# Hash attention and token/channel mixer on one core: where the second group of hash products of the first pair stands

## The chip, the cores and the metric

The kernel runs on one core of a Trainium2 chip. The metric is the device time of one execution in microseconds (us); the time before is the median of three runs, and the profile comes from one further execution. The engines are named as in the profile: PE is TensorE (PEld its weight loads), DVE is VectorE, ACT is ScalarE, POOL is GpSimd, SP is SyncE, which here only issues transfers.

## The reference

Attention with a hash mask over 4 batches, 8 heads, 768 positions and 64 channels per head, then a mixer over tokens and channels. A query sees a key only if all six signs of their projections agree:

```python
q_bits = (np.einsum('bhsd,dk->bhsk', q, proj) > 0).astype(np.int64)
k_bits = (np.einsum('bhsd,dk->bhsk', k, proj) > 0).astype(np.int64)
...
mask = q_bucket[:, :, :, None] == k_bucket[:, :, None, :]
scores = scale * np.matmul(q, k.transpose(0, 1, 3, 2))
scores = np.where(mask, scores, -1000000000.0)
scores = scores - np.max(scores, axis=-1, keepdims=True)
attn = np.exp(scores)
attn = attn / (np.sum(attn, axis=-1, keepdims=True) + 1e-09)
return np.matmul(attn, v).astype(np.float32)
...
h = np.maximum(xt @ w_tok1, 0.0) @ w_tok2
u = x + h.transpose(0, 2, 1)
h2 = np.maximum(u @ w_ch1, 0.0) @ w_ch2
return (u + h2).astype(np.float32)
```

## The kernel before

The program has three stages, one after the other: attention (to about 310 us in the profile), the token mixer, and the channel mixer, which takes more than half of the time. Each stage is written out by hand in the order in which its instructions are to stand in the engines' queues; no scheduler moves them. The change touches only the beginning of the attention.

Attention goes over 16 pairs: a pair is two heads of one batch, whose 64 channels each fill the 128 rows of the array, head i in rows 64i to 64i + 63. Queries are taken in two halves of 384 (class `Half`), keys in six blocks c of 128. For a half and a block, `product` (L350) makes the scores of both heads in one PSUM tile `sc`, of which there are three: the plain products of q and k in float32, and the bits products, which add a large negative number wherever the hashes of query and key differ. `exponential` (L358) then takes the exponential on ACT. The loop at L367 keeps its order by hand: within a half the plain products of a block come first and its bits products after. In the very first half (`first` is true) the plain products of blocks 0 and 1 are both issued before the bits products of block 0: block 0 is put on the list `waiting` and the loop goes on.

The bits come from hash products. From pair 1 on, `hashes(n)` (L292) makes them a pair ahead and moves them into place by DMA. For pair 0 there is no pair ahead, so `first_hashes(half)` (L318) makes them in place: four products of 32 columns (eight passes on TensorE, since float32 goes in two), then on DVE one comparison (L330), one scaling of the key bits (L331) and two comparisons that put the query bits in the rows of their heads (L334). `first_hashes(0)` reads positions 0 to 383 of q and k, which hold key blocks 0 to 2 and the queries of the first half. `first_hashes(1)` reads positions 384 to 767, which hold key blocks 3 to 5 and the queries of the second half. Both were issued at L365, ahead of all score products. They write to two different PSUM tiles (`acc` for the first, `sm` for the second).

The loads of pair 0 are three transfers on SP's queue (L271, twice, for the first half of k and of q; L272 for the second half of both), then follow the load of pair 1 (L268), the values of pair 0 (L280, L282) and a first piece of a weight (L169). Before any product on data stand twelve small products on constants (L469), whose result isn't used. An engine takes its instructions in order: one that waits for a load holds up those behind it.

Of the kernel before, what the change touches and what calls it, by code (L numbers as in the profile page):

```python
# [48 lines left out]
def kernel(  # L49
# [208 lines left out]
    def attention(pool, psum, W1, W2, x0):  # L258
# [59 lines left out]
        def first_hashes(half):  # L318

            sl = slice(HALF * half, HALF * half + HALF)  # L320
            ps = psum.tile([P, 512], F32, name="hw", tag="sm" if half else "acc", bufs=1)[:, :HALF]
            for i in range(2):
                for which in (1, 0):
                    at = D * i + 32 * (1 - which)
                    nc.tensor.matmul(  # L325
                        ps[at : at + 32], projwide[:, D * i : D * i + 32], loaded[0][0][:, which, sl],
                        start=True, stop=True,
                    )
            q, k = (bitrows[0][:, which, sl] for which in range(2))
            nc.vector.tensor_scalar(k, ps, 0.0, 0.5, op0=ALU.is_gt, op1=ALU.subtract)  # L330
            nc.vector.tensor_scalar(k, k, widescale, None, op0=ALU.mult)  # L331
            for i in range(2):
                at = D * i
                nc.vector.tensor_scalar(  # L334
                    q[at : at + 32], ps[at + 32 : at + 64], 0.0, 0.5, op0=ALU.is_gt, op1=ALU.subtract,
                )

        class Half:
# [5 lines left out]
            def scores(self):  # L344

                qkt, bits = loaded[self.n][0], bitrows[self.n % 2]
                qs = slice(HALF * self.half, HALF * self.half + HALF)
                first = self.n == self.half == 0

                def product(sc, t, c, start):  # L350
                    for i in range(2):
                        rows = slice(D * i, D * i + D)
                        nc.tensor.matmul(  # L353
                            sc[:, i, :HALF], t[rows, 1, P * c : P * c + P], t[rows, 0, qs],
                            start=start, stop=not start,
                        )

                def exponential(sc):  # L358
                    e = pool.tile([P, 2, HALF], F32, name="e", tag="e", bufs=12)
                    nc.scalar.activation(e, sc[:, :, :HALF], ACT.Exp, scale=SCALE)  # L360
                    self.es.append(e)

                waiting = []
                if first:
                    for half in range(2):  # L365
                        first_hashes(half)
                for c in range(NR):  # L367
                    sc = psum.tile([P, 2, 512], F32, name="sc", tag="sc", bufs=3)
                    if c == self.half == 0 and not first:
                        product(sc, bits, c, True)  # L370
                        product(sc, qkt, c, False)
                        exponential(sc)
                        continue
                    product(sc, qkt, c, True)
                    waiting.append((c, sc))
                    if first and c == 0:
                        continue
                    for c, sc in waiting:
                        product(sc, bits, c, False)
                        exponential(sc)  # L380
                    waiting = []
# [1092 lines left out]
```

## Time and profile before

| | us |
|---|---|
| median of three runs | 797.34 |
| the three runs | 796.74 to 799.93 |
| the profiled execution, its own time | 795.77 |
| its span, first to last instruction | 794.0 |
| scores of one half, both heads, on TensorE (six blocks) | 4.9 |
| one pair in the attention, pitch of the chain | 18.97 |
| exponential of one block, on ACT (L360) | 0.811 |

The span is shorter than the execution's own time by the 1.8 us that lie around the first and last instruction. The half's 4.9 us are half of the 9.80 us that the chain gives to 12 blocks of one pair, and the pitch is the distance of two such pieces (44.92 less 25.96, in us from the start of the span). Times in the profile are counted from the span's start. A row of the timeline stands for a run of like instructions, with its start, its length, its engine and line, and in brackets the idle time of the engine before it with what ended it. Matmuls overlap, so one row may begin before the row ahead of it has ended.

### The profile page before, as it was taken

Reading aid. Unit: us, or ns where it says so; the run is one execution under the profiler, and the core shown is the slowest. Engines: PE = TensorE matmul, PEld = TensorE weight load, DVE = VectorE, ACT = ScalarE, POOL = GpSimd, SP = SyncE. Lnnn points to the kernel's source line nnn. Section 1 sums busy time; section 2 is a strip of 40 time slices with the busy share of each in tenths; the row PEclk is TensorE's granted clock in tenths of the full one; section 3 lists DMA queues with packets and bytes.
Section 4 is the critical chain, followed back from the end, with each engine's and each line's share of the span. In section 5 each row is a group of like instructions: output and inputs, shape, how many; then the busy total and the mean of one; then the engine's idle time right before and its main releaser. Section 6 shows DMA issues by size and latency. Waiting matters only on the chain.

```text
span 794.0 us, 12166 instructions
## 1 busy us (share of the span) xinstructions
PE 786.4 (99%) x4661; PEld 464.9 (59%) x4661; DVE 659.7 (83%) x885; ACT 441.4 (56%) x706; POOL 53.5 (7%) x77
## 2 busy tenths in 40 slices
PE   8999999999999999999999999999999999999997
PEld 4444444444444444455544458876667886666886
DVE  5989898988987677999688788988769897778986
ACT  6688888888888886333323221327773335775111
POOL 1000000000000000011121010111110012000001
PEclk9999999999999999999999999999999999999999
DMA  4435353538352425796726994699754578730456
GB/s 163 163 123 163 123 163 123 163 122 246 143 178 87 154 47 166 215 281 173 175 60 228 334 356 145 185 294 283 218 148 139 217 204 195 218 109 1 148 176 159
DMA packets 90974, 138.67 MB, mean 175 GB/s; under 512 B 29656, under 2 KB 63392, under 8 KB 88608
## 3 DMA queue, kind: packets, MB, share of 16 engines
q1 hardware_dynamic: 82752, 112.86, 42.9%
q0 software_dynamic: 7728, 24.64, 14.0%
q8 instruction: 38, 0.62, 0.3%
q10 hardware_dynamic: 432, 0.34, 0.2%
q14 instruction: 24, 0.20, 0.1%
HBM read 97.21 MB, written 33.16 MB: 164 GB/s over the span
## 4 chain that ended last, share of the span: by engine, by line
PE 99%; DMA 1%; SPq 0%; DVE 0%; issue 0%
PE b L779 50%; PE sc L353 20%; PE acc L406 16%; PE t L652 5%; PE t L692 5%; PE sums L430 2%; PE hp L301 1%; DMA qk<-in_qk 1%; PE hw L325 0%; SPq L271 0%; DVE second L1202 0%; PE b L1319 0%; SPq L1469 0%
## 5 line engine op out<-in xcount | busy, mean ns | idle before, releaser
L360 ACT ACTIVATE e<-sc 128x768 f32<-128x768 f32 x192 | 154.1, 811 | 11.6 <-PE sc L353 11.2
L353 PE MATMUL sc<-qk 64*128 64x384 f32 x768 | 152.6, 483 | 0.0
L779 PE MATMUL b<-R,second 128*128 128x256 f32 (+1 forms) x612 | 150.9, 404 | 0.0
L779 PEld LDWEIGHTS b<-R,second 128*128 128x128 f32 x612 | 116.3, 190 | 31.6 <-issue 17.2
L785 ACT COPY c<-b 128x512 f32<-128x512 f32 (+1 forms) x78 | 37.4, 488 | 169.2 <-PE b L779 159.6
L406 PE MATMUL acc<-e,vn 128*32 128x384 f32 x1536 | 127.0, 486 | 0.0
L391 DVE TENSOR_TENSOR esd<-esd,e 128x768 f32<-128x768 f32 x96 | 92.0, 958 | 10.4 <-ACT e L360 0.5
L406 PEld LDWEIGHTS acc<-e,vn 128*32 128x32 f32 x1536 | 49.9, 110 | 73.9 <-issue 73.3
L353 PEld LDWEIGHTS sc<-qk 64*128 64x128 f32 x768 | 68.2, 187 | 40.8 <-issue 35.6
L779 PE MATMUL b<-XT,WC 128*128 128x256 f32 (+1 forms) x264 | 82.5, 456 | 0.0
L779 PEld LDWEIGHTS b<-XT,WC 128*128 128x128 f32 x264 | 50.2, 190 | 29.6 <-issue 25.1
L353 PE MATMUL sc<-bits 64*128 64x384 bf16 x384 | 62.5, 323 | 0.0
L387 DVE SCALAR_TENSOR_TENSOR esd<-e 128x768 f32<-128x768 f32 x32 | 30.6, 955 | 24.5 <-ACT e L360 24.5
L652 PE MATMUL t<-x,W 128*128 128x512 f32 x96 | 41.8, 593 | 0.0
L353 PEld LDWEIGHTS <-bits 64*128 64x128 bf16 x384 | 18.7, 94 | 33.0 <-issue 9.0
L712 POOL DMA_DIRECT2D XT<-second x8 | 9.9, 1232 | 386.0 <-DVE second L711 361.6
L451 ACT COPY rec<-rec 32x384 f32<-32x384 f32 x64 | 32.6, 510 | 5.0 <-DVE rec L445 4.2
L412 ACT ACTIVATE num<-acc,vsum 128x384 f32<-128x384 f32 x32 | 18.6, 581 | 29.8 <-PE acc L406 29.4
L779 PE MATMUL b<-XT,SW 128*128 128x256 f32 (+1 forms) x120 | 34.6, 422 | 0.0
L779 PE MATMUL b<-TA,WC 128*128 128x512 f32 x72 | 33.8, 592 | 0.0
L779 PE MATMUL b<-TA,SW 128*128 128x512 f32 x72 | 32.9, 592 | 0.0
L394 DVE TENSOR_TENSOR esd<-esd,e 128x768 f32<-128x768 f32 x32 | 30.5, 954 | 1.9
(217 smaller groups left out, 1129.3 us busy)
## 6 DMA issues: line engine op xcount, KB each, us to landing
second<-left SPq DMA_DIRECT2D x18, 1344.0 KB
raw<-in_moe_w_ch SPq DMA_DIRECT2D x16, 768.0 KB
qk<-in_qk SPq DMA_DIRECT2D x15, 768.0 KB
seen<-in_qk POOLq DMA_DIRECT2D x21, 384.0 KB, 3.8
WC<-hidden_left SPq DMA_DIRECT2D x15, 448.0 KB
vn<-in_v SPq DMA_DIRECT2D x16, 384.0 KB
vt<-in_vT SPq DMA_DIRECT2D x16, 384.0 KB
x<-bounced SPq DMA_DIRECT2D x4, 1536.0 KB
```

The costliest lines, as they stand in the source:

```text
L353: nc.tensor.matmul(sc[:, i, :HALF], t[rows, 1, P * c : P * c + P], t[rows, 0, qs], start=start, stop=not start,)
L360: nc.scalar.activation(e, sc[:, :, :HALF], ACT.Exp, scale=SCALE)
L387: nc.vector.scalar_tensor_tensor(self.d, es[0], NR * EPS, es[1], op0=ALU.add, op1=ALU.add,)
L391: nc.vector.tensor_tensor(self.d, self.d, e, op=ALU.add)
L394: nc.vector.tensor_tensor(self.d, self.d, self.es[-1], op=ALU.add)
L406: nc.tensor.matmul(acc[D * i + d : D * i + d + 32], vn[:, i, c, d : d + 32], e[:, i], start=(c == 0), stop=(c == NR - 1),)
L412: nc.scalar.activation(nums[self.n][:, self.half], acc, ACT.Identity, scale=-1.0, bias=vsum,)
L451: nc.scalar.copy(rec[other : other + 32, h], rec[at : at + 32, h])
L652: nc.tensor.matmul(ps, W1[:, r, P * j : P * j + P], x[:, r], start=(r == 0), stop=(r == NR - 1),)
L692: nc.tensor.matmul(ps[at], left, right, start=start, stop=True, skip_group_check=True,)
L779: nc.tensor.matmul(ps, left(k), right(k), start=start and k == ks[0], stop=stop and k == ks[-1], skip_group_check=True,)
L785: nc.scalar.copy(c, ps)
```

## The change

In the first half of pair 0, `first_hashes(0)` stays where it was, and `first_hashes(1)` is called in the loop when block 1 is at hand, after the plain products of blocks 0 and 1 and ahead of the bits products of block 0. All other calls stay as they were.

```diff
                 waiting = []
                 if first:
-                    for half in range(2):
-                        first_hashes(half)
+                    first_hashes(0)
                 for c in range(NR):
                     sc = psum.tile([P, 2, 512], F32, name="sc", tag="sc", bufs=3)
...
                     waiting.append((c, sc))
                     if first and c == 0:
                         continue
+                    if first and c == 1:
+                        first_hashes(1)
                     for c, sc in waiting:
                         product(sc, bits, c, False)
                         exponential(sc)
```

## The prediction

> **What bounds the kernel now.** I read the page's busy times first, then the list of waits for TensorE, then the chain that ended last, and last the timeline of the first ten microseconds, where the change lies.
>
> The page's first part, busy time per engine with its share of the span:
>
> ```profile
> PE 786.4 (99%) x4661; PEld 464.9 (59%) x4661; DVE 659.7 (83%) x885; ACT 441.4 (56%) x706; POOL 53.5 (7%) x77
> ```
>
> TensorE is busy 786.4 us of a 794.0 us span. Outside its work lie 7.6 us, so nothing that only fills its idle time can bring more than 1% here. Where those idle times are, the list of waits says (engine, line, what was waited for, total us, times, longest). Asked for TensorE over the whole span, it has two entries:
>
> ```profile
> PE hw L325 <- DMA qk<-in_qk: 1.3, 1, 1.3
> PE idle L469 <- DVE ones L97: 1.1, 1, 1.1
> ```
>
> The second is the start of the program. The first is the one wait for data that TensorE has in the whole kernel: the hash products of line 325 wait 1.3 us for a load of q and k. The chain that ended last, asked for its first 60 us, goes through the same place (start, us, what):
>
> ```profile
> 1.77 4.55 DMA qk<-in_qk
> 6.33 0.14 issue
> 6.47 0.85 PE hw L325 x8
> 7.32 10.12 PE sc L353 x72
> 17.44 0.78 PE hp L301 x8
> 18.22 7.74 PE acc L406 x96
> ...
> 35.76 0.78 PE sums L430 x8
> 36.54 0.65 PE hp L301 x8
> ```
>
> From 6.47 on the chain is TensorE alone; before that it is the third load of pair 0, both operands' second half, issued at 1.77 and landed at 6.33. The work that follows is handed on without a gap, so whatever comes off ahead of 8.6 us should come off the end. The timeline of the first ten microseconds shows who could have worked in between (start, us, engine, line, operation, and in brackets the idle time before it):
>
> ```profile
> 3.84 1.34 PE L325 MATMUL hw<-qk,projs 128*32 128x384 f32 x8
> ...
> 5.24 0.56 DVE L330 TENSOR_SCALAR bits<-hw 128x384 bf16<-128x384 f32 x1 [3.80 <-PE hw L325]
> 5.91 0.32 DVE L331 TENSOR_SCALAR bits<-bits,widescale 128x384 bf16<-128x384 bf16 x1
> 6.26 1.14 DVE L334 TENSOR_SCALAR bits<-hw 32x384 bf16<-32x384 f32 x2
> ...
> 6.47 0.85 PE L325 MATMUL hw<-qk,projs 128*32 128x384 f32 x8 [1.29 <-DMA qk<-in_qk]
> ...
> 7.25 1.56 PE L353 MATMUL sc<-qk 64*128 64x384 f32 x8
> 7.44 0.56 DVE L330 TENSOR_SCALAR bits<-hw 128x384 bf16<-128x384 f32 x1
> ...
> 8.64 0.49 PE L353 MATMUL sc<-bits 64*128 64x384 bf16 x4
> ...
> 9.04 9.25 ACT L360 ACTIVATE e<-sc 128x768 f32<-128x768 f32 x12 [6.49 <-PE sc L353]
> ```
>
> The reader is to see that the products of the first half end at 5.18 (3.84 + 1.34), that TensorE then stands still until 6.47, and that the plain products of key blocks 0 and 1 (7.25 on) need only the first halves, which the first hash products at 3.84 have already read.
>
> **What the Trainium skill says.** "TensorE: Matmul & The Clock Gate", Part 3, What overlaps and what doesn't: matmuls keep their program order in start and end, and a weight load overlaps a matmul in flight only if it goes to other rows of the array. So a matmul that waits for a load holds up everything behind it, as the 1.29 us show; and a change between full-height hash products and half-height score products cannot be quite seamless. The trace agrees: the same four hash products of line 301 take 0.78 us on the chain where they follow score products (17.44) and 0.65 where they follow the sums (36.54), so a change-over is about 0.13. The same page, Part 1, What's actually happening, says that the array begins at half its clock and is released after about 3.4 us of activity, in a window that runs free of the kernel. Here line 325's matmuls last 482 to 849 ns, the long ones in the first group, which fits a clock that rose during that group, near 4 to 5 us; but the granted clock is given as 1.00 for every stretch of the first ten microseconds, so the trace has no line for the moment itself.
>
> **The change, part by part.** No instruction is added or taken away. On TensorE's queue the four hash products of the second half (eight passes, 0.85 us) step behind the four plain products of blocks 0 and 1 (eight passes). On DVE, ACT, GpSimd and SP the order stays the same; no DMA issue moves in its queue. The waits are the same ones: the second hash products still wait for the third load, the bits products for DVE.
>
> *Removed: the stall.* The plain products follow the first hash products. Before, they started 0.07 ahead of the end of the hash products (7.25 against 6.47 + 0.85 = 7.32); the same overlap after the first group gives 5.18 - 0.07 = 5.11. They hold the array for 8.64 - 7.25 = 1.39, to 6.50.
>
> *Moved: the second hash products.* Their load landed at 6.33 and they could start at 6.47, so at 6.50 the wait is over: the moved work is almost exactly as long as the stall (1.39 against 1.29 plus the 0.07 overlap). One change-over from score to hash products, 0.13, puts them at 6.63. They hold TensorE for 7.25 - 6.47 = 0.78, to 7.41. The change-over is bounded by nothing (then 7.28) and by the 0.63 us that the weight queue was idle at the first score products after the hash products (then 7.91); 0.13 is the same pair of operations in the same direction, so I take it.
>
> *The next wait: the bits of the first half.* DVE starts on them at 5.24 as before and ends at 6.26 + 1.14 = 7.40. In the kernel before, the bits products came at 8.64, so this had a cover of 1.24 us; now the cover is gone. With 0.06 from an end to the engine that waits for it (5.18 to 5.24) the second head can start at 7.46. The first head needs only the first of the two L334, done near 6.83. So DVE and TensorE's own queue arrive together, and I put the bits products of block 0 at 7.5. Gain: 8.64 - 7.5 = 1.14; rounded, 1.1.
>
> *Behind the waiting bits product* stand all later score products, and ACT's first exponential, which comes 9.04 - 8.64 = 0.40 after it; it moves from 9.04 to 7.9. Nothing else on TensorE could run there.
>
> *The second half's bits.* Their products end at about 7.45 against 7.32 before, so DVE is at them from 7.5 on and has the key bits (0.56 + 0.32 and gaps, 0.91) at about 8.45. They are wanted by block 3: bits products 0 and 1 at 7.5 take 0.33, block 2 takes 0.81, and block 3's plain products 0.65, to about 9.4 with the short wait for the exponential that frees its buffer. 0.9 us of cover remain; if it went, what is late would be added one for one. The query bits of that half are needed only in the half after, at about 12.
>
> *What lies further on.* The exponentials take 811 ns against 806 of TensorE's products per block, and their start moves with the bits products. The value loads of pair 0, the weights and the load of pair 1 share the DMA engines until about 11.5; the first that is used is wanted at 17.4 - 1.1 = 16.3. The eight bit transfers for pair 1 follow from hash products that move with the rest. I find nothing held to the clock on the wall, so I carry the lead of 1.1 us to the end at full size.
>
> *Sum.* The profiled execution took 795.77 us, 794.0 of it the span: 795.77 - 1.1 = 794.67. The median of the three timed runs is 797.34, 1.57 above the profiled one; the same edit is worth the same there: 797.34 - 1.1 = 796.2, or 0.14% less. About 0.5% (4.0 us) is what a measurement of this kernel can tell from no change, and the three runs alone are spread over 3.19 us.
>
> **The rivals.**
>
> - *As worked out, 796.2.* For it: one wait, work of equal length that needs nothing new. With the change-over at its two bounds the gain is 1.18 (DVE then decides) and 0.7; chance 0.68.
> - *The clock is still low under the moved products, 796.8.* They now start 2.1 us earlier. If the rate rose at 6.5 in place of during the first hash products, the 1.39 us until 6.5 do half of their work, the rest takes 0.7 to 7.2, then 0.13 + 0.78 leads to 8.1, a gain of 0.5. Against it: the profiled execution had the full rate by the end of the first group. Chance 0.12.
> - *The lead is taken back later, 797.3.* A transfer that already ran as fast as it could, in the later stages where DMA slices reach 0.9, would let TensorE arrive 1.1 us early and wait for it. For it: transfers next to full there. Against it: the list of waits shows none on TensorE after 6.47, and each load is released by work that moves too. Chance 0.12.
> - *No gap to fill, only the change-over, slower: 797.6.* The mechanism is the landing of the first halves. If in the timed executions they land so late that the first hash products end at 6.2 or later rather than at 5.18, second halves close behind, TensorE has no stall there; the kernel before then has its bits products held up by DVE or by the same products as the one after, and what is left is two change-overs more, 2 x 0.13 = 0.26 us. It decides from about 1.0 us of delay between the two loads. Against it: the stall is 1.29 in the trace that is there, and the second load can hardly land with the first, being queued behind it. Chance 0.08.
>
> That the edit doesn't do what it says I leave out: the order of instructions on TensorE shows the exchange and no other.
>
> **How the numbers follow.** The likeliest gives 796.2. Its own bounds (gain 0.7 to 1.3) make 796.0 to 796.6; the rivals reach to 797.6. Wider than all of these is the spread of the runs themselves, 796.74 to 799.93 with a profiled one at 795.77, and a median of a few runs can lie 1.5 us to either side of the value worked out. So the range is 794.6 to 798.4. No case reaches 0.5% (793.4 or 801.3): all lie within it, and what I leave to both sides is for something that the profile doesn't show: faster 0.02, same 0.95, slower 0.03.
>
> **What would show it.** In the profile after: the plain products at 5.1 with no idle time before them; the second hash products at 6.5 to 6.7 without a wait on the load; bits products at 7.4 to 7.6 and the first exponential at 7.9; the later products of line 301 at 16.3 rather than 17.4, and the last stages about 1.1 us earlier. A wait of line 325 for the load still there, matmuls of line 353 twice as far apart near 5.1, a new wait of TensorE after 300 us, or bits products later than 8.2 would show one of the other cases. The forecast is wrong if the time differs from before by 4 us, or if the span's start is no shorter than now.

## The result, and the profile after

The changed kernel takes 796.50 us in the median of 22 runs (794.69 to 798.11), the kernel before 797.49 in 22 (795.88 to 799.93). The ratio is 0.9982 with a 95% interval of 0.9974 to 0.9989: faster by 1.4 us, between 0.9 and 2.1. The medians alone are 0.99 us apart; eight of the 22 runs before lie above 798.4 us and none of those after. The difference is inside the 0.5% that the prediction took for no change, but with 22 runs a side it is clear of zero, and the median is near the forecast of 796.2.

The profiled execution took 795.47 us with a span of 793.7. TensorE's list of waits, asked over the whole span, now has one entry (engine, line, what was waited for, total us, times, longest); the wait for the load is gone:

```profile
PE idle L470 <- DVE ones L97: 1.1, 1, 1.1
```

The timeline of its first ten microseconds (start, us, engine, line, operation, idle time before it):

```profile
3.84 1.70 PE L325 MATMUL hw<-qk,projs 128*32 128x384 f32 x8
...
5.47 1.99 PE L353 MATMUL sc<-qk 64*128 64x384 f32 x8
5.60 0.56 DVE L330 TENSOR_SCALAR bits<-hw 128x384 bf16<-128x384 f32 x1 [4.16 <-PE hw L325]
...
6.62 1.14 DVE L334 TENSOR_SCALAR bits<-hw 32x384 bf16<-32x384 f32 x2
...
7.40 0.85 PE L325 MATMUL hw<-qk,projs 128*32 128x384 f32 x8
...
8.19 0.50 PE L353 MATMUL sc<-bits 64*128 64x384 bf16 x4
```

The plain products now follow the first hash products, and TensorE has no idle time ahead of the second ones. But the bits products came at 8.19, only 0.45 ahead of the 8.64 of before, and not at 7.5. The eight plain passes are what is long: from their start at 5.47 to the hash products at 7.40 lie 1.93 us, where the kernel before had 1.39 from 7.25 to 8.64, and the row itself reads 1.99 against 1.56. The first hash products also took 1.70 against 1.34. So TensorE's passes were slow for longer in this execution than in the profiled one of before. Whether that belongs to the change is what two profiles cannot say.

The end of the chain (start, us, what) shows that the lead was carried through the kernel. Before, its last two TensorE pieces:

```profile
752.40 0.11 PE b L1319
752.51 36.28 PE b L779 x168
```

and after:

```profile
751.86 0.11 PE b L1320
751.97 36.28 PE b L780 x168
```

That is 0.54 us earlier at 752 us, for 0.45 at 8 us. The span is only 0.3 shorter: from the end of the last piece (751.97 + 36.28 = 788.25) to the end of the span DVE's last additions and the transfers out took 5.4 us, before 5.2.

### The profile page after: what moved, and what is told of

Its sections match the earlier page's. It is cut to its first block, busy times and chain, and to the rows that moved or that the text cites. A ratio compares the mean times of both kernels' runs of the same rounds, so it can differ in the third digit from the quotient of the medians.

```text
span 793.7 us, 12166 instructions
## 1 busy us (share of the span) xinstructions
PE 787.1 (99%) x4661; PEld 464.9 (59%) x4661; DVE 660.0 (83%) x885; ACT 441.6 (56%) x706; POOL 53.5 (7%) x77
## 4 chain that ended last, share of the span: by engine, by line
PE 99%; DVE 0%; issue 0%; DVEq 0%
PE b L780 50%; PE sc L353 20%; PE acc L407 16%; PE t L653 5%; PE t L693 5%; PE sums L431 2%; PE hp L301 1%; PE idle L470 0%; PE hw L325 0%; DVE second L1203 0%; DVE ones L97 0%; PE b L1320 0%; DVEq L1470 0%
## 5 line engine op out<-in xcount | busy, mean ns | idle before, releaser
L353 PE MATMUL sc<-qk 64*128 64x384 f32 x768 | 153.1, 484 | 0.0
L353 PEld LDWEIGHTS sc<-qk 64*128 64x128 f32 x768 | 68.4, 188 | 41.8 <-issue 36.7
L353 PE MATMUL sc<-bits 64*128 64x384 bf16 x384 | 62.5, 323 | 0.0
L353 PEld LDWEIGHTS <-bits 64*128 64x128 bf16 x384 | 18.5, 94 | 33.2 <-issue 8.8
```

What stands on the lines that cost most here:

```text
L353: nc.tensor.matmul(sc[:, i, :HALF], t[rows, 1, P * c : P * c + P], t[rows, 0, qs], start=start, stop=not start,)
```

## The experiments

Two theories stood. *Useful work*: the gain is the plain products put into the stall, and nothing else matters. *Clock*: what also counts is how long TensorE works at a low rate at the start, either by chance from execution to execution, or because an idle stall makes the low rate last. The ratios are against the kernel before, run on the same chip beside each experiment. Line numbers shift by a few between the kernels: L469, L470 and L472 are the same line, and so are L325 and L324, or L353 and L352.

**Both kernels profiled again.** No edit. e1 and e2 were timed as well; e8 and e12 are one profiled execution each.

> The kernel before, unchanged, timed against itself and profiled a second time. If only the stall matters, its times form one group near 797.5 us (ratio 0.999 to 1.001) and its profile again has a wait of about 1.3 us of the second hash products for the load, with plain products 1.39 us long. If the rise of TensorE's clock is also at work, the times form two groups, near 796.9 and 798.8 us, and the profile shows hash or plain products of another length than the first profile of before had (8 plain passes anywhere from 1.4 to 2.7 us).

> The changed kernel, unchanged, profiled a second time. Both theories: 0.998 of before, within 0.001. If the clock explains why the bits products came at 8.19 us in the first profile of after and not at 7.5, a second profile may show another position between 7.4 and 8.9 us, and it goes with the length of the eight plain passes (1.4 to 2.7 us): bits products at about 5.1 or 5.5 plus that length plus 0.8 to 0.9. If the late arrival has another cause, the plain products are again 1.9 us long.

> The kernel before once more, for a third profile of its start. If the clock decides, position of the first bits products and time go together: bits products at 8.6 us with a time near 797 us, or at 9.5 to 10.5 us with a time near 799. If only the stall matters, bits products at 8.64 us within 0.1.

> The kernel before once more, for a fourth profile. If what follows the start takes the same time in every execution, the last product of TensorE ends 780.0 to 780.5 us after the first bits product, as in three profiles of before. If a wait in the token stage is what makes its slow executions, the difference is 781 to 782 us and the list of waits shows the token products waiting for ACT.

e1 against the same kernel gave 1.0012 (1.0000 to 1.0024; median 798.12 in 17 runs): a median of one copy can lie 0.1% off, which bounds what any ratio below can carry. Its plain products are 1.39 long, as in the first of its two cases, and its first hash products 1.09 against 1.34, as in the second; its times are spread from 796.14 to 800.56 without two clear groups. e2 gave 0.9989 (0.9982 to 0.9996; median 796.27). The start of e2, timeline:

```profile
3.84 1.04 PE L325 MATMUL hw<-qk,projs 128*32 128x384 f32 x8
...
4.80 1.56 PE L353 MATMUL sc<-qk 64*128 64x384 f32 x8
...
5.96 1.14 DVE L334 TENSOR_SCALAR bits<-hw 32x384 bf16<-32x384 f32 x2
...
6.39 0.85 PE L325 MATMUL hw<-qk,projs 128*32 128x384 f32 x8
...
7.17 0.50 PE L353 MATMUL sc<-bits 64*128 64x384 bf16 x4
```

and of e12, the fourth profile of before:

```profile
3.84 1.17 PE L325 MATMUL hw<-qk,projs 128*32 128x384 f32 x8
6.88 0.85 PE L325 MATMUL hw<-qk,projs 128*32 128x384 f32 x8 [1.87 <-DMA qk<-in_qk]
7.67 1.56 PE L353 MATMUL sc<-qk 64*128 64x384 f32 x8
9.06 0.49 PE L353 MATMUL sc<-bits 64*128 64x384 bf16 x4
```

In e2 the plain row is again 1.56 long and the bits products stand at 7.17, 1.0 ahead of the first profile of the same kernel and ahead of the 7.4 that had been put as the earliest. Nothing in the program differs, so the late 8.19 there was the length of the early passes in that execution: of the 1.02 us, 0.67 lie in the first hash products (5.47 less 4.80) and 0.34 in the plain ones (1.93 against 1.59). In e12 the load lands later than in the first profile, and every start after it is later by the same 0.4. All six profiles (us; the last column is the own time of the profiled execution):

| | first hash products, length | second, start | bits products | last TensorE piece ends, after the bits products | time |
|---|---|---|---|---|---|
| before | 1.34 | 6.47 | 8.64 | 780.15 | 795.77 |
| before, e1 | 1.09 | 6.20 | 8.38 | 780.51 | 796.34 |
| before, e8 | 1.72 | 6.74 | 8.92 | 780.00 | 795.86 |
| before, e12 | 1.17 | 6.88 | 9.06 | 780.15 | 797.32 |
| after | 1.70 | 7.40 | 8.19 | 780.06 | 795.47 |
| after, e2 | 1.04 | 6.39 | 7.17 | 780.67 | 796.27 |

Before, the start of the bits products follows the load: it is 2.17 to 2.18 after the second hash products in all four, whatever the first ones took. After, it follows the length of the early passes. The means are 8.75 and 7.68, a lead of 1.07; at the end of the last TensorE piece they are 788.95 and 788.05, a lead of 0.90. What lies between takes 780.0 to 780.7 in all six, as e12 was to test. The transfers after the last piece take 5.2 to 6.7, which is why e2, with the earliest start and TensorE done first of the six (787.84), has not the shortest time: its tail is 6.7. Position at the start and time do not go together from one execution to the next: e8 has 8.92 and 795.86, which fits neither of the two cases expected of it. They do so in the mean. e2 also has one late wait of TensorE that the other five lack, for a transfer:

```profile
PE b L780 <- DMA second<-left: 0.2, 1, 0.2
```

The profiles come from more than one chip. The length of the first hash products varies on a single one as well: e1 to e4, all on one chip and alike up to there, read 1.09, 1.04, 1.67 and 1.62. How much of the spread of the landing belongs to the chip is not separated.

**Only block 0 ahead (e4).**

```diff
                     if first and c == 0:
+                        first_hashes(1)
                         continue
-                    if first and c == 1:
-                        first_hashes(1)
```

> Only the plain products of block 0 ahead of the second hash products, those of block 1 behind. Useful work in the stall at full clock: half of it is used, the second hash products again wait about 0.6 us for the load, bits products near 8.0 us, gain about 0.65 us (ratio 0.9992). Where the clock rises late, the plain products of block 0 are slow enough to fill the stall, and the gain is that of the whole change, 1.0 to 1.4 us (0.9982 to 0.9988).

0.9986 (0.9978 to 0.9994; median 796.04 in 13 runs): no loss against the whole change is seen, though the interval holds both the 0.9992 of the first case and the 0.9982 to 0.9988 of the second. Its timeline shows why half the work was enough in that execution:

```profile
3.84 1.62 PE L325 MATMUL hw<-qk,projs 128*32 128x384 f32 x8
5.39 0.93 PE L353 MATMUL sc<-qk 64*128 64x384 f32 x4
6.25 0.85 PE L325 MATMUL hw<-qk,projs 128*32 128x384 f32 x8
7.03 0.92 PE L353 MATMUL sc<-qk 64*128 64x384 f32 x4
7.78 0.49 PE L353 MATMUL sc<-bits 64*128 64x384 bf16 x4
```

The first hash products took 1.62, and the plain products of one block, 0.86 us from 5.39 to 6.25, were enough to reach the landing (second hash products start between 6.20 and 6.88 in the profiles of before). The gain is that of the second case, but not for its reason: the plain products were not slow (0.93 for block 0, 0.92 for block 1 after it). It was the first hash products that were long, and the load had landed by 6.25, so that little of the stall was left to fill. What happens where the first hash products are short, no profile of e4 shows. The experiment doesn't show that the second block's products are needed in the stall.

**One step further back (e5).** The second hash products behind the bits products of blocks 0 and 1.

```diff
-                    if first and c == 1:
-                        first_hashes(1)
                     for c, sc in waiting:
                         product(sc, bits, c, False)
                         exponential(sc)
+                    if first and waiting[-1][0] == 1:
+                        first_hashes(1)
                     waiting = []
```

> The second hash products one step further back, behind the bits products of blocks 0 and 1. If the wait for DVE is what comes next after the stall, TensorE now waits for the bits of the first half (ready about 7.4 to 7.8 us) from the end of the plain products (6.5 us at full clock, 7.4 at a late one), the first exponential comes as early as in the changed kernel or earlier, and the whole is 0.4 to 0.9 us slower than the changed kernel, so 0.1 to 1.0 us faster than before (ratio 0.9988 to 0.9999). If DVE is no limit, it equals the changed kernel (0.9982).

0.9983 (0.9973 to 0.9993; median 796.46). The wait that was expected is there, in the timeline:

```profile
6.80 0.32 PE L353 MATMUL sc<-bits 64*128 64x384 bf16 x1 [0.20 <-DVE bits L334]
...
7.39 0.48 PE L353 MATMUL sc<-bits 64*128 64x384 bf16 x3 [0.27 <-DVE bits L334]
...
8.59 0.92 PE L353 MATMUL sc<-qk 64*128 64x384 f32 x4
```

TensorE waits twice for DVE's L334, and the plain products of block 2 start at 8.59, against 7.51 in e2; 0.23 of that is the longer first hash products (1.27 against 1.04). So DVE is next in line after the stall, as the forecast had it, and the changed order is the place where its bits are just ready: in e2 L334 ends at 7.10 and the bits products start at 7.17. But the loss of 0.4 us or more against the changed kernel does not appear in the times; the medians are 796.46 here and 796.50 and 796.27 there. In the profiles TensorE's last piece ends at 788.47 here, and at 788.25 and 787.84 there. Why the medians don't show a loss is open, and which of the two orders is better is left undecided by these runs.

**The stall filled with work that isn't used (e3, e9).** Six small products in e3, three in e9, in the order of before.

```diff
-                    for half in range(2):
-                        first_hashes(half)
+                    first_hashes(0)
+                    fill = psum.tile([P, 2, 512], F32, name="fill", tag="sc", bufs=3)
+                    for _ in range(6):
+                        nc.tensor.matmul(fill[:D, 0, :D], ones, ones, start=True, stop=True)
+                    first_hashes(1)
```

> The order of before, with six small products on constants (twelve passes, result unused) issued between the two groups of hash products, so that TensorE is active in most of the stall and does no useful work there. If the gain is only useful work put into the stall: no gain, ratio 1.000 within 0.001, or up to 0.4 us slower where the small products outlast the stall. If activity in the stall also makes the clock rise sooner in part of the executions: about 0.5 to 1.0 us faster than before (0.9988 to 0.9994), and no times above 798.4 us, where before has 8 of 22.

> As the filled stall, with three small products in place of six (six passes, about 0.8 us at a low clock, 0.4 at a high one), so that they end before the load lands and cost nothing. If activity alone keeps the clock from rising late: faster than before by 0.3 to 0.7 us in the median (0.9991 to 0.9996) and no time above 799 us. If only useful work counts: 1.000 within 0.0007, with some times above 799 us as before has them.

e3: 1.0004 (0.9998 to 1.0011; median 797.68). e9: 1.0002 (0.9993 to 1.0011; median 797.91). Being active in the stall brings nothing in the median; it has to be the work that is due. That is for the first theory, and the gain of 0.3 to 1.0 us that the second had forecast for the two did not come. One sign is for the second: none of the 35 runs of e3 and e9 took over 798.86 us, where 29 of all 186 timed runs of the kernel before lie above 799 (up to 801.22), and of 43 of the changed kernel none is above 798.11. The same holds for e4 and e5 (highest 797.15 and 798.24), where the stall is filled as well. So the changed order may save something in such runs that the worked-out sum doesn't contain. The upper runs of before were not caught in a profile, so what makes them is open. In both filled profiles TensorE also has a wait that none of the six above has; e9's list of waits:

```profile
PE t L695 <- ACT second L700: 1.4, 1, 1.4
PE idle L472 <- DVE ones L97: 1.1, 1, 1.1
PE hw L325 <- DMA qk<-in_qk: 0.3, 1, 0.3
```

The chain of e9 near 378 us shows what stands behind the first line: a transfer in the token mixer, on which ACT and then TensorE wait.

```profile
378.70 8.61 DMA XT<-second
...
387.39 0.49 ACT second L700
...
387.92 2.20 PE t L695 x6
```

It costs 1.4 us there, 1.3 in e3, 0.2 in e5, and in e6 below, which fills nothing, it is the longest:

```profile
PE t L692 <- ACT second L697: 1.6, 1, 1.6
```

So the filling isn't needed for it. None of the six profiles of the two main kernels has this wait on TensorE's list. In the filled kernels it may hide a small gain; what brings it about is open.

**The twelve small products at the start taken away but one (e6, e7).**

```diff
-        for _ in range(12):
+        for _ in range(1):
```

> The kernel before with one of the twelve small products on constants at the start in place of twelve. If activity in the first microseconds raises the clock, it now rises after 7 us: hash and plain products take about twice as long (plain 2.7 us), and the kernel is 1.0 to 3.5 us slower than before (1.0012 to 1.0045). If the clock has no part, no change (1.000 within 0.0005).

> The changed kernel with one small product at the start in place of twelve. If the clock has no part: 0.998 as the changed kernel. If it has: slower than the changed kernel by 0.8 to 3 us. If what the exchange brings is useful work in the stall, it stays ahead of the cold kernel before by 0.8 to 1.4 us, since the stall for the load stays the same length.

e6 (order of before): 1.0024 (1.0014 to 1.0034; median 799.63). e7 (changed order): 0.9992 (0.9980 to 1.0005; median 797.52). So the start's activity is worth about 2 us to the one and about 1 us to the other, and between the two lie 2.1 us by the medians, more than the 0.8 to 1.4 expected. The profiles have 1.82 of lead at the bits products (11.57 less 9.75); e6's has the 1.6 us in the token mixer besides, which e7's has not. e6, timeline:

```profile
3.80 1.89 PE L325 MATMUL hw<-qk,projs 128*32 128x384 f32 x8 [2.23 <-DMA qk<-in_qk]
7.41 1.51 PE L325 MATMUL hw<-qk,projs 128*32 128x384 f32 x8 [1.73 <-DMA qk<-in_qk]
8.85 2.93 PE L353 MATMUL sc<-qk 64*128 64x384 f32 x8
11.57 0.61 PE L353 MATMUL sc<-bits 64*128 64x384 bf16 x4
```

and e7:

```profile
5.58 2.93 PE L353 MATMUL sc<-qk 64*128 64x384 f32 x8
8.44 1.38 PE L325 MATMUL hw<-qk,projs 128*32 128x384 f32 x8
9.75 0.50 PE L353 MATMUL sc<-bits 64*128 64x384 bf16 x4
```

The same eight plain passes that took 1.56 now take 2.93. In e7 they do so while TensorE would have waited for the load, so the slow passes cost less; in e6 they come after the wait, at 8.85, and are still slow.

**The second load later (e10, e11).** Its issue moved behind the load of pair 1, in the order of before (e10) and in the changed one (e11).

```diff
-                nc.sync.dma_start(out=t[:, :, HALF:], in_=qk[b, hp, :, :, HALF:])
...
         load_qk(1)
+        nc.sync.dma_start(out=loaded[0][0][:, :, HALF:], in_=qk[0, 0, :, :, HALF:])
```

> The kernel before with the load of the second half issued after the load of pair 1 rather than ahead of it, so it lands later by about the time that 768 KB take (about 1.9 us at the 410 GB/s of that stretch). If the stall is set by this load: the wait in line 325 grows from 1.3 to about 3.2 us, bits products at about 10.5 us, 1.9 us slower than before (ratio 1.0024). If something else sets it, no change.

> The changed kernel with the same later load. Its plain products still cover 1.4 us (full clock) to 2.7 us (low clock) of the wait: a wait of 0.9 to 1.9 us for the load appears, bits products at about 9.2 us. If the gain is the plain products put into the stall, it stands ahead of the kernel before with the late load by 1.3 to 1.4 us, and is 0.5 us slower than the kernel before (1.0003 to 1.0010). If the gain depended on the stall being about as long as the moved work, the lead would be smaller than 1 us or gone.

e10: 1.0066 (1.0053 to 1.0079; median 802.41, 6 runs). e11: 1.0024 (1.0014 to 1.0033; median 798.94, 21 runs). Both lost more than expected: e10 5.0 us by the medians, where 1.9 had been put, and e11 1.5, where 0.5 had been put. Timeline of e10:

```profile
3.84 1.73 PE L324 MATMUL hw<-qk,projs 128*32 128x384 f32 x8
9.27 1.50 PE L324 MATMUL hw<-qk,projs 128*32 128x384 f32 x8 [3.70 <-DMA qk<-in_qk]
10.70 2.86 PE L352 MATMUL sc<-qk 64*128 64x384 f32 x8
13.40 0.49 PE L352 MATMUL sc<-bits 64*128 64x384 bf16 x4
```

and of e11:

```profile
5.64 1.99 PE L352 MATMUL sc<-qk 64*128 64x384 f32 x8
8.87 0.85 PE L324 MATMUL hw<-qk,projs 128*32 128x384 f32 x8 [1.24 <-DMA qk<-in_qk]
9.65 0.50 PE L352 MATMUL sc<-bits 64*128 64x384 bf16 x4
```

The load sets the stall: later by 2.8 us in e10 (6.47 to 9.27), it delays the second hash products by as much. But the lead of the changed order over the other is not 1.4 us; it is 3.5 by the medians and 3.75 at the bits products (13.40 less 9.65). 0.40 of the 3.75 is the landing (9.27 and 8.87). The work put into the wait is 1.39 at the full rate. The rest is slow passes after it: e10 spends 10.70 - 9.27 = 1.43 on its hash products where e11 spends 0.78 (0.65 more), and 2.70 on the plain ones instead of 1.39 (1.31 more). 0.40 + 1.39 + 0.65 + 1.31 = 3.75. Early products and loads are the same in both, and the medians say that it is no chance of one execution: the idle 3.7 us is what goes with the slow passes. This speaks for the clock theory, at a stall two to three times as long as the one in question. In the four profiles of before, with stalls of 1.2 to 1.9 us, the passes after the stall were quick each time (second hash products 0.85, plain 1.56). The length of the stall isn't all, though: in e6, with one small product at the start, passes were slow after 1.73 us, and in e9 the second hash products were slow in part after 0.3 (1.07 against 0.85).

## Why the prediction was right

*The stall, its cause and what goes into it*: right. TensorE's wait for the third load went away, no order on another queue changed, and e10 shows that the load's landing sets its end.

*The sum*: right in the mean, with terms that e2 lets one read at the full rate. The plain products started at 4.80, 0.08 ahead of the end of the first hash products (3.84 + 1.04 = 4.88; 0.07 was put). They held TensorE for 6.39 - 4.80 = 1.59, so the change-over, put at 0.13, was 0.20. The second hash products held it for 0.78, exactly as put. The bits products then came at 7.17; the working put them at 7.5 because its first hash products ended at 5.18 rather than 4.88. The gain, put at 1.14, is 1.07 in the mean of the profiles at the start, 0.90 at the last product, and 0.99 by the medians of the first comparison. That one profile of before led so near to the mean is in part luck: it lay in the middle of its kind (8.64, mean 8.75), while single pairs of a profile before and one after differ by 0.19 to 1.89 us. And the upper bound of 1.3 that stands in the range isn't the working's own, which is 1.18.

*The next wait*: right. DVE and TensorE arrive together (7.10 and 7.17 in e2; in the first profile of after DVE is done 0.43 ahead, 7.76 and 8.19), and one step further back TensorE does wait for DVE (e5). Its price in the times did not show.

*The lead is carried to the end*: right for TensorE's work, 780.0 to 780.7 us in six profiles. The rival that it is taken back later is not what happened; of its sign, a new wait of TensorE after 300 us, e2 has 0.2. But two places are now known where single executions lose up to 1.6 us: a transfer in the token mixer near 378 us (seen in the variants only) and the transfers after the last product.

*The rival of the low clock*: given as a case of its own with 0.12, it is what the first profile of after shows. It was worked out as bits products at 8.1 and a gain of 0.5; the profile has 8.19 and 0.45. The mistake in the working was to take the moment at which TensorE becomes quick from one profile, as if it belonged to the kernel: by the first hash products' length (1.04 to 1.72 us with the same work) it differs between executions of the same program. The Trainium skill, "TensorE: Matmul & The Clock Gate", Part 1, What's actually happening, says of the window over which activity is counted that it doesn't start with the kernel and that the moment of the rise varies; the profiles agree with that, but the clock that the profile shows as granted reads 1.00 even over stretches such as e6's 8 to 11.8 us, where passes took about twice their time, so it is the lengths of passes that show it here. That it is the clock which makes them slow is the page's account, not a reading of these traces.

*The rival on the slower side*: its condition, a first load so late that no stall is left, was met in none of the profiles.

*The number*: the measured 796.50 lies 0.3 above the forecast, and well inside the range, which was that wide for the spread of the runs.

## What to carry to other kernels

A wait for a load near the start of a program is worth filling with products that are due and need only what has landed; filled with products nobody needs it gave nothing. How far the moved work helps is read from three ends that have to be worked out together: the landing, the engine that prepares the next operand, and the rate at which TensorE runs at that moment. Before a fraction of a microsecond at the start is read from two profiles, the start should be profiled several times, for one program's start differed by 1.0 us between two of its own.

## What was not expected of the hardware

Products on real data after an idle stall were slow again or still: eight plain passes took 2.86 us (e10) after an idle 3.7 us, and 1.56 after 1.2 to 1.9 us in the kernel before; with only one small product at the start they took 2.93 after 1.73 us (e6). The landing of the same load, issued at 1.77 or 1.78 us each time, moved the second hash products between 6.20 and 6.88 us in four profiles of one kernel. And what follows the last product, 0.8 us of additions on DVE and then transfers, took between 5.2 and 6.7 us with the same data, a spread of more than the 1.0 us between the medians.
